# One more chunk of a feed-forward layer by seven products, on weights scaled a second time, with a new table of orders

## The chip, the cores and the metric

The kernel runs on one core of a Trainium2 chip. The metric is the device time of one execution in microseconds (us). Before the change the median of 3 runs is 268.34 us (267.95 to 268.7).

A core has engines that run side by side, each with its own list of instructions in a fixed order: TensorE (PE in the profile; its weight loads are listed apart as PEld), VectorE (DVE), ScalarE (ACT), GpSimd (POOL) and SyncE (SP), whose list here starts the DMA transfers. An engine takes the next instruction of its list only when the semaphores that this instruction names have been raised by the others. So an instruction that waits holds back everything behind it on its engine.

## The reference

Four layers work on an activation x of 2048 tokens by 512 features, in bf16: attention A, feed-forward B, then A and B again with the same weights.

```python
def _A_ref(x, wqkv, wo):                       # D = 512, 32 heads of 16
    q, k, v = ...                              # x @ wqkv, split into heads
    phi = lambda t: jnp.where(t > 0, t + 1, jnp.exp(t)) + 1e-6
    pq, pk = phi(q), phi(k)
    kv = jnp.einsum("bhsd,bhse->bhde", pk, v)
    z = jnp.einsum("bhsd->bhd", pk)
    num = jnp.einsum("bhqd,bhde->bhqe", pq, kv)
    den = jnp.einsum("bhqd,bhd->bhq", pq, z)[..., None] + 1e-6
    return ... (num / den) @ wo

def _B_ref(x, w1, w2):                         # w1 512 x 1376, w2 1376 x 512
    return jnp.maximum(x @ w1, 0) @ w2

x = x + _A_ref(_layernorm(x), wqkv, wo)        # layer 0
x = x + _B_ref(_layernorm(x), w1, w2)          # layer 1
x = x + _A_ref(_layernorm(x), wqkv, wo)        # layer 2
x = x + _B_ref(_layernorm(x), w1, w2)          # layer 3
```

The layer norm has no weights; it subtracts the mean and divides by the root of variance + 1e-5.

## The kernel before

**Tiles.** The 2048 tokens are 16 tiles of 128 (`i`), and four tiles are a chunk (`t`, 0 to 3). The 1376 hidden features are ten blocks of 128 and a rest of 96. Block `c` (0 to 4) and block `c + 5` make a block pair. PSUM, where PE writes, has eight banks of 128 x 512 f32; `alloc_bank` takes one for a piece of work. The buffer `big` is cut into units of 128 x 512 bf16: hidden features of one block and chunk, or scaled queries and their divisors in the attention layers.

**An attention layer** first takes, per chunk, keys times values (`kproj`, the features phi on ACT and DVE, then the products `g` of tokens), and at its end, called the bar here, it folds these into one matrix `Mf` per half (`GT`, `KVT`, `Mf` are the steps), computes the divisors ("dens", `ps<-big,Zc` in the profile, 32 rows), takes their reciprocal on ACT (`lnd`, `rdc`), spreads them over the rows by DMAs (`spread`, L893), multiplies the queries by them on DVE (`pqs`, L899), and multiplies by `Mf` (`fin`, `ps<-Mf,big`; the first ones are `ps<-Mf,xres`). `resid` (L748 on DVE) adds the result to x and gives the row sums; ACT squares (L754); POOL turns the sums into the layer norm's factors; DVE or ACT writes the normed tile (`norm`, L644 and L652). Then a transposing DMA started by SP (L660, `tr`) puts the chunk's rows into `Tb`, where PE reads them. The first chunk's rows are transposed by PE itself (`trp`) and copied out of PSUM by `trev`.

**A feed-forward layer** computes per chunk the hidden features (`b_h`), then sums of them (`feature_sums`, L1183 on DVE), then the output (`b_out`). The output is computed for two token tiles and two column halves together by seven products in place of eight (Strassen's idea in Winograd's form: sums of blocks are multiplied, and the seven results are added up in PSUM): class `_Pair`, with `product(k)` for k = 1 to 7, five matmuls of 256 columns each. The sums of `w2` that it needs are made once (`weight_sums`, L1152).

For the hidden features there are two forms. The plain form (`b_h_plain`) takes four matmuls of 512 columns per block, bf16. The seven-product form (`b_h_halves`) takes a block pair and the chunk's two token halves together: seven products `hp{t}_{c}_{k}` of two matmuls of 256 columns each, in f16, with sums of token blocks (`tsum`, L1031) and of weight blocks (`sw`, L1010). Product 1 goes into half a bank `Y`, product 5 into its other half; ACT copies both (`hc` into the bank `R`, `hm` into `escr`, both L1065); DVE adds the second copy to later products (half adds `ha`, L1068); a relu per block ends it (L1121 on ACT or L1122 on DVE). Which chunks take this form says `H16`: before, chunks 2 and 3 of layer 1 and all of layer 3. `H_PLAIN` gives the number of block pairs of such a chunk that stay plain.

**The weights of the f16 form.** f16 has a smaller range than bf16, so `scale_find` takes a bound of the weights and finds a power of two; `scale_weights` multiplies `w1` by it in place (`wsc0` to `wsc3`, L1003 on DVE or L1004 on ACT, each 128 x 1376) and makes the four sums `sw`. Being in place, this comes after the last plain product that reads `w1` unscaled. Residuals undo the factor.

**What sets the order.** The program adds operations one by one with what they read and write, a list of steps interleaves each layer with the next (a step names the chunk it needs and the one it provides), and `_list_schedule` then sets each engine's list before the program is built: among the next few operations of each engine it takes the one that can start first by a table of costs (`C_*`). The order in which operations are looked at is their number plus what the table `HINTS` adds for them. An operation with two forms (`add_flex`) goes to the engine that is done with it first by those costs. `OPEN_H`, `OPEN_OUT` and `ALLOC_AT` say how far one unit of seven products may start before the one ahead of it.

## Time and profile before

| what | value |
|---|---|
| median of 3 runs | 268.34 us (267.95 to 268.7) |
| the profiled execution | 267.63 us, of which 265.9 are the span |
| TensorE (PE) busy | 259.5 us, 98%, 1872 matmul records |
| VectorE (DVE) busy | 215.2 us, 81%, 555 instructions |
| ScalarE (ACT) busy | 193.7 us, 73%, 422 instructions |
| GpSimd (POOL) busy | 50.8 us, 19%, 131 instructions |
| DMA | 23.22 MB |

Rows of the profile read: line, engine, operation, out<-in by the program's names, shape, count, then busy time and the mean of one in ns, then the idle time of the engine ahead of them and what ended it. Rows of a timeline begin with the start and the duration in us of a run of like instructions. Rows of the chain begin in the same way and name the piece of work that the end of the program was followed back to. Layer 0 ends and layer 1 begins about 52.8 us into the span, layer 2 has its bar from 171 to 183 us, and layer 3 begins at about 194 us.

### The profile page before, as it was taken

To read this page: it belongs to the slowest core of one execution; us is meant where nothing else is said; L and a number is where in the kernel's file an instruction comes from. 1 tells how busy PE (TensorE), PEld (TensorE's weight loads), DVE (VectorE), ACT (ScalarE), POOL (GpSimd) and SP (SyncE) were. 2 spreads that over 40 slices of the span, in tenths; PEclk is the share of its full clock that TensorE was granted. 3 is DMA by queue.
4 is the path that set the end of the run, shared out by engine and by line. 5 is a ranking of instruction groups with operands and counts; after the bars stand their busy time and mean duration, and the time that the engine had idled before them with its cause. 6 is when DMAs were issued, how large, how long until landed. Compare 5 with 4: busy or idle time off the path is not lost.

```text
span 265.9 us, 5093 instructions
## 1 busy us (share of the span) xinstructions
PE 259.5 (98%) x1872; PEld 171.0 (64%) x1890; DVE 215.2 (81%) x555; ACT 193.7 (73%) x422; POOL 50.8 (19%) x131
## 2 busy tenths in 40 slices
...
GB/s 215 258 83 91 245 177 328 129 187 70 58 153 81 0 22 62 47 72 1 2 0 0 72 35 53 4 143 118 99 110 31 99 2 39 119 23 65 36 1 160
DMA packets 48666, 23.22 MB, mean 87 GB/s; under 512 B 38816, under 2 KB 46976, under 8 KB 48640
## 3 DMA queue, kind: packets, MB, share of 16 engines
...
q14 instruction: 11, 0.09, 0.1%
...
## 4 chain that ended last, share of the span: by engine, by line
PE 83%; DVE 6%; DMA 5%; POOL 2%; ACT 1%; issue 1%; SPq 1%; POOLq 0%; DVEq 0%
PE ps L722 83%; DMA wqkv<-in_A_wqkv_dram 4%; DVE xres L748 3%; DMA Tb<-xn 1%; DVE big L899 1%; POOL rstd L629 1%; DVE xn L644 1%; SPq L536 0%; ACT sqscr L754 0%; DVE wqkv L738 0%; DVE KVT L824 0%; POOL mean L619 0%; DVE xres L899 0%; POOL veps L627 0%; DVE big L712 0%
## 5 line engine op out<-in xcount | busy, mean ns | idle before, releaser
L1121 ACT ACTIVATE big<-ps 128x512 bf16<-128x512 f32 x62 | 35.8, 599 | 14.6 <-PE ps L722 14.1
L722 PE MATMUL ps<-Tb,w 128*128 128x256 f16 (+2 forms) x240 | 41.9, 301 | 0.0
L754 ACT ACTIVATE sqscr<-xres 128x512 bf16<-128x512 f32 x48 | 30.0, 626 | 10.7 <-DVE xres L748 10.2
L722 PE MATMUL ps<-w,big 128*128 128x256 bf16 (+5 forms) x212 | 35.8, 293 | 0.1
L722 PE MATMUL ps<-wqkv,Tb 128*128 128x512 bf16 x137 | 33.2, 379 | 1.0 <-DMA wqkv<-in_A_wqkv_dram 0.7
L704 ACT ACTIVATE big<-ps 128x512 bf16<-128x512 f32 x48 | 28.9, 606 | 5.3 <-PE ps L722 4.9
L722 PE MATMUL ps<-big,xn 128*128 128x512 bf16 (+1 forms) x155 | 30.1, 335 | 0.4 <-issue 0.2
L722 PE MATMUL ps<-xn,xin 128*128 128x256 f16 x168 | 29.9, 272 | 0.0
L722 PEld LDWEIGHTS ps<-Tb,w 128*128 128x128 f16 (+1 forms) x240 | 23.1, 98 | 9.5
L1068 DVE TENSOR_TENSOR ps<-ps,escr 128x256 f32<-128x256 f32 x56 | 23.2, 427 | 4.7 <-PE ps L722 4.6
L722 PE MATMUL ps<-Tb,wqkv 128*128 128x512 bf16 x112 | 26.9, 379 | 0.0
L706 ACT ACTIVATE escr<-ps 128x512 bf16<-128x512 f32 x44 | 26.0, 610 | 1.2 <-PE ps L722 1.2
L619 POOL TENSOR_SCALAR mean<-s 128x4 f32<-128x4 f32 (+1 forms) x13 | 4.0, 305 | 117.5 <-DVE xres L748 117.4
L722 PE MATMUL ps<-Mf,big 128*128 128x512 bf16 x108 | 24.5, 379 | 0.3
L722 PEld LDWEIGHTS ps<-wqkv,Tb 128*128 128x128 bf16 x144 | 13.8, 98 | 15.7 <-DMA wqkv<-in_A_wqkv_dram 1.2
L722 PEld LDWEIGHTS ps<-w,big 128*128 128x128 bf16 (+1 forms) x213 | 20.4, 98 | 5.0
L722 PEld LDWEIGHTS ps<-big,xn 128*128 128x128 bf16 x160 | 15.2, 98 | 12.8 <-issue 0.8
L722 PE MATMUL ps<-xin,big 128*128 128x256 bf16 x150 | 20.8, 272 | 0.0
L708 DVE TENSOR_SCALAR escr<-escr 128x512 bf16<-128x512 bf16 x52 | 14.6, 288 | 7.4 <-ACT escr L706 7.3
L715 DVE TENSOR_TENSOR big<-big,escr 128x512 bf16<-128x512 bf16 x46 | 19.0, 419 | 0.7 <-ACT big L704 0.2
L722 PEld LDWEIGHTS ps<-Mf,big 128*128 128x128 bf16 x112 | 10.7, 98 | 12.7 <-DVE big L899 0.3
L722 PEld LDWEIGHTS ps<-Tb,wqkv 128*128 128x128 bf16 x112 | 10.8, 98 | 11.4 <-DVE xres L748 0.2
(141 smaller groups left out, 494.8 us busy)
## 6 DMA issues: line engine op xcount, KB each, us to landing
...
```

The source lines that it names most:

```text
L619: g.add(POOL, lambda e: e.tensor_scalar(mean[:, sl], s1[:, sl], -INV_D, None, ALU.mult), [("s1", i) for i in tl], [("mean", i) for i in tl ...
L629: g.add(POOL, lambda e: e.tensor_tensor(rstd[:, sl], veps[:, sl], nhalf[:, 0:hi - lo], ALU.pow), [("veps", lo), ("nhalf",)], [("rstd", i) ...
L644: ts = (POOL, lambda e: e.tensor_scalar(dst, src, mean[:, i:i + 1], rstd[:, i:i + 1], ALU.add, ALU.mult), C_POOL_NORM)
L704: g.add(ACT, lambda e: e.activation(dst_ap, psv[:, b, :], ACTF.Identity, bias=1.0 + 1e-6, scale=sc), [("ps", b)] + rk, [dst_key], C_ACT_PS ...
L706: g.add(ACT, lambda e: e.activation(esc, psv[:, b, :], ACTF.Exp, scale=sc), [("ps", b)] + rk, [ekey], C_ACT_EXP + xd, name=name + "_exp")
L708: g.add(DVE, lambda e: e.tensor_scalar(esc, esc, 1.0, 1e-6, ALU.min, ALU.add), [ekey], [ekey], C_DVE_BF4X, name=name + "_em")
L715: g.add(DVE, lambda e: e.tensor_tensor(dst_ap, dst_ap, esc, ALU.max), [dst_key, ekey], [dst_key], 340.0, name=name + "_phi")
L722: last = e.matmul(o, l, r, start=st, stop=sp, skip_group_check=skip)
L748: g.add(DVE, lambda e: e.scalar_tensor_tensor(xres[:, i, :], psv[:, b, :], 0.0 if sc is None else sc, src, ALU.add if sc is None else ALU. ...
L754: g.add(ACT, lambda e: e.activation(sqscr[:, q, :], xres[:, i, :], ACTF.Square, accum_out=s2[:, i:i + 1]), [("xres", i)], [("sqscr", q), ( ...
L1068: g.add(DVE, lambda e: e.tensor_tensor(psv[:, bank, 256:512], psv[:, Y, 0:256], m5, ALU.add), [("ps", Y), ("escr", s)], [("ps", bank)], C_ ...
L1121: g.add_flex([(ACT, lambda e: e.activation(unit_ap(u), psv[:, b, :], ACTF.Relu), C_ACT_PSUM), (DVE, lambda e: e.tensor_scalar(unit_ap(u), ...
```

## The change

1. Chunk 1 of layer 1 takes the seven-product form in block pairs 0, 1 and 2; pairs 3 and 4 of it stay plain (with f16 inputs).
2. Its products need scaled weights while chunk 0 still reads the unscaled ones. A new function `scale_early` therefore writes a second, scaled copy of `w1` into units of `big` that hold nothing yet: those of chunks 2 and 3, for blocks 0 to 4 and 5 to 9, and unit 44 for the rest. It has four operations `wse` (two weight rows by five blocks of 128 each, L1049 of the new code) and one for the rest (`wser`, L1056), each for DVE or ACT. The sums `sw` are now made from this copy (L1064), ahead of chunk 0's output. The four in-place scalings `wsc` stay; all are now on DVE, where before DVE and ACT had two each.
3. The step that computes the hidden features of chunk 1 now waits in the interleaving for the last chunk of layer 0.
4. The limits `OPEN_H`, `OPEN_OUT` and `ALLOC_AT` go. Product 1 of a unit now stands behind product 5 of the unit ahead of it, in both forms, and product 5 of a hidden unit claims `R` as well.
5. `HINTS` is a wholly new table, so every engine's order changes in all layers.

In instructions: 24 matmuls of 512 columns go, 42 of 256 come. DVE gets 6 half adds, 4 token sums, 2 in-place scalings, 4 `wse` and one copy of transposed rows out of PSUM at the start, and loses 6 relus and a norm. ACT gets 6 relus, 3 `hc`, 3 `hm` and `wser`, and loses 2 in-place scalings. Lines of the code move by 12 at the front (L722 becomes L734, L748 L760) and by up to 58 further on.

The order at three places. First SP's list from the program's start, its DMA starts (`xin` is x, `wqkv` the weights; L546 is the half-matrix wq, loaded in two parts). Before:

```order
L536 DMA xin<-in_A_x_dram 128x512
L536 DMA xin<-in_A_x_dram 128x1536
L542 DMA wqkv<-in_A_wqkv_dram 128x2x512 x2
L546 DMA wqkv<-in_A_wqkv_dram 128x2x512
L536 DMA xin<-in_A_x_dram 128x1024
L536 DMA xin<-in_A_x_dram 128x2048
L536 DMA xin<-in_A_x_dram 128x1024
L536 DMA xin<-in_A_x_dram 128x2048
L546 DMA wqkv<-in_A_wqkv_dram 128x2x512
L660 DMA_TRANSPOSE Tb<-xn 128x8x128 x4
```

Now:

```order
L548 DMA xin<-in_A_x_dram 128x512
L548 DMA xin<-in_A_x_dram 128x1536
L554 DMA wqkv<-in_A_wqkv_dram 128x2x512 x2
L548 DMA xin<-in_A_x_dram 128x1024
L558 DMA wqkv<-in_A_wqkv_dram 128x2x512 x2
L548 DMA xin<-in_A_x_dram 128x1024
L548 DMA xin<-in_A_x_dram 128x2048 x2
L672 DMA_TRANSPOSE Tb<-xn 128x8x128 x4
```

The second part of wq (L546 before, L558 now) has moved from behind all loads of x to the place behind its first part, and both loads of 128x2048 stand after it.

Second, PE's list in chunk 1 of layer 1 (`w` is `w1` or `w2`, `tw` a sum of `w2`, `xin` holds sums of `w1` and `w2`, `xn` sums of features or tokens, `Tb` transposed rows). Before, from the tail of the list that overlaps the end of layer 0's output:

```order
L722 MATMUL ps<-Tb,w 128x512 x8
L722 MATMUL ps<-w,Tb 128x96 x16
L722 MATMUL ps<-Tb,w 128x512 x36
L722 MATMUL ps<-w,big 128x256 x5
L722 MATMUL ps<-tw,xn 128x256 x5
```

Now:

```order
L734 MATMUL ps<-Tb,w 128x512 x4
L734 MATMUL ps<-Tb,big 128x256 x2
L734 MATMUL ps<-Tb,big 128x512 x12
L734 MATMUL ps<-xn,xin 128x256 x2
L734 MATMUL ps<-big,Tb 128x96 x16
L734 MATMUL ps<-Tb,big 128x512 x4
L734 MATMUL ps<-Tb,big 128x256 x2
L734 MATMUL ps<-w,Tb 128x96 x16
L734 MATMUL ps<-w,big 128x256 x5
L734 MATMUL ps<-tw,xn 128x256 x5
```

The products from the second copy (`Tb,big`) and from sums (`xn,xin`) now begin among the plain blocks, and go on between the output products of chunk 0 that follow.

DVE's list ahead of that place, before (L748 residuals, L644 norms, L1122 relus, L1152 sums of `w2`, L1183 feature sums, L1031 token sums):

```order
L748 SCALAR_TENSOR_TENSOR xres,s<-ps,xin 128x512 x2
L644 TENSOR_SCALAR xn<-xres,mean,rstd 128x512 x2
L1122 TENSOR_SCALAR big<-ps 128x512 x3
L748 SCALAR_TENSOR_TENSOR xres,s<-ps,xin 128x512
L644 TENSOR_SCALAR xn<-xres,mean,rstd 128x512 x2
L1122 TENSOR_SCALAR big<-ps 128x512 x2
L1152 TENSOR_TENSOR tw<-w 128x1280
L1152 TENSOR_TENSOR xin<-w,tw 128x1280
L644 TENSOR_SCALAR xn<-xres,mean,rstd 128x512 x2
L1183 TENSOR_TENSOR xn<-big 128x1280
```

Now (L760 residual, L656 norms, L1049 the second copy, L1064 sums of it, L1040 in-place scalings, L1087 token sums):

```order
L760 SCALAR_TENSOR_TENSOR xres,s<-ps,xin 128x512
L656 TENSOR_SCALAR xn<-xres,mean,rstd 128x512 x3
L1036 TENSOR_SCALAR pw<-pw 128x1
L1035 TENSOR_SCALAR pw<-pw 128x1
L1049 TENSOR_SCALAR big<-w,pw 128x2x5x128 x2
L656 TENSOR_SCALAR xn<-xres,mean,rstd 128x512 x3
L1049 TENSOR_SCALAR big<-w,pw 128x2x5x128 x2
L1064 TENSOR_TENSOR xin<-big 128x1280
L1064 TENSOR_TENSOR xin<-xin,big 128x1280
L1040 TENSOR_SCALAR w<-w,pw 128x1376
L1087 TENSOR_TENSOR xn<-Tb 128x512
```

The relus and the feature sums that stood between the norms have made room for the second copy and its sums.

Third, PE's list at the bar of layer 2 (`big,Zc` 32 rows are the dens; `big,xn` token products; `Tb,wqkv` projections; `GT,wqkv` and `wo,KVT` the way to `Mf`). Before:

```order
L722 MATMUL ps<-ident,GT 128x1 x4
L722 MATMUL ps<-big,xn 128x512 x4
L722 MATMUL ps<-big,Zc 32x512 x12
L722 MATMUL ps<-big,xn 128x256 x8
L722 MATMUL ps<-Tb,wqkv 128x512 x4
L722 MATMUL ps<-big,xn 128x512 x4
L722 MATMUL ps<-GT,wqkv 128x128 x2
L722 MATMUL ps<-big,xn 128x256 x8
L722 MATMUL ps<-GT,wqkv 128x128 x4
L722 MATMUL ps<-Tb,wqkv 128x512 x4
L722 MATMUL ps<-GT,wqkv 128x128 x8
```

Now:

```order
L734 MATMUL ps<-ident,GT 128x1 x4
L734 MATMUL ps<-big,xn 128x256 x4
L734 MATMUL ps<-GT,wqkv 128x128 x2
L734 MATMUL ps<-big,Zc 32x512 x12
L734 MATMUL ps<-GT,wqkv 128x128 x2
L734 MATMUL ps<-big,xn 128x512 x8
L734 MATMUL ps<-GT,wqkv 128x128 x4
L734 MATMUL ps<-Tb,wqkv 128x512 x4
L734 MATMUL ps<-GT,wqkv 128x128 x6
L734 MATMUL ps<-Tb,wqkv 128x512 x4
L734 MATMUL ps<-wo,KVT 128x512 x2
```

The dens stand behind four narrow token products in place of four wide ones, and the steps towards `Mf` are spread between the token products that come after them.

The diff, cut to its core (of the table `HINTS` one line each):

```diff
-H16 = {(1, 2), (1, 3), (3, 0), (3, 1), (3, 2), (3, 3)}
+H16 = {(1, 1), (1, 2), (1, 3), (3, 0), (3, 1), (3, 2), (3, 3)}
-ALLOC_AT = 5
-OPEN_OUT = 99
-OPEN_H = 99
-H_PLAIN = {(3, 0): 2}
+H_PLAIN = {(1, 1): 2, (3, 0): 2}
-HINTS = {"0.apos": 38, "0.as_h1": -183, "0.as_h2": 580, ...
+HINTS = {"0.ainvs": 93, "0.apos": 224, "0.apows": 243, ...
...
+        def early(t):
+            return g.layer == 1 and t == 1
+
+        def w1_of(t):
+            if early(t):
+                return lambda d, c: big[:, 512 * we_unit(c) + 128 * d:512 * we_unit(c) + 128 * d + min(128, DFF - 128 * c)].bitcast(F16)
+            w = w1h if h16(t) else w1
+            return lambda d, c: w[:, d, 128 * c:min(128 * c + 128, DFF)]
+
+        def we_unit(c):
+            return 44 if c == NFC - 1 else NCH * (c % HN5) + 2 + c // HN5
+
+        def we_ap(half, d0, d1):
+            v = big[:].bitcast(F16).rearrange("p (c t d k) -> p c t d k", t=NCH, d=4, k=128)
+            return v[:, 0:HN5, 2 + half, d0:d1, :].rearrange("p c d k -> p d c k")
...
+        def scale_early():
+            for half in range(2):
+                for d in (0, 2):
+                    i_ = w1[:, d:d + 2, HD * half:HD * half + HD].rearrange("p d (c k) -> p d c k", k=128)
+                    o_ = we_ap(half, d, d + 2)
+                    g.add_flex([(DVE, lambda e, i_=i_, o_=o_: e.tensor_scalar(o_, i_, pw[:, 1:2], None, ALU.mult), C_DVE_SC),
+                                (ACT, lambda e, i_=i_, o_=o_: e.activation(o_, i_, ACTF.Copy, scale=pw[:, 1:2]), C_ACT_ABS)],
+                               [("pws",), ("w1",)], [("we", half, d)] + we_keys(half), name="wse%d%d" % (half, d))
...
-            add(1, lo[:, :, l], hi[:, :, l], ALU.add, W1S)
-            add(3, lo[:, :, f], lo[:, :, l], ALU.subtract, W1S[0:2])
...
+            add(1, ll, hl, ALU.add, [("we", 1, 0), ("we", 1, 2)] + we_keys(1))
+            add(3, lf, ll, ALU.subtract, [("we", 0, 0), ("we", 1, 0)] + we_keys(0) + we_keys(1))
...
                     op = mm_group(..., 
-                             rd + wk, [("ps", bank)], 2 * C_MM256, "hp%d_%d_%d" % (t, c, k))
-                    if k == 1 and len(h_open) >= OPEN_H:
-                        op.odeps.append(h_open[-OPEN_H])
-                    if k == 2:
-                        h_open.append(op)
+                             rd + wk, [("ps", bank)] + ([("ps", R)] if k == 5 else []), 2 * C_MM256, "hp%d_%d_%d" % (t, c, k))
+                    if k == 1:
+                        op.odeps.extend(h_open)
+                    if k == 5:
+                        h_open[:] = [op]
...
                 def h_step(t):
+                    if layer == 1 and t == 1:
+                        scale_early()
                     b_h(t, 2 if t == 0 else 1)
...
                 for t in range(NCH):
-                    steps.append((t, None, lambda t=t: h_step(t)))
+                    steps.append((NCH - 1 if layer == 1 and t == 1 else t, None, lambda t=t: h_step(t)))
                     if t >= 1:
-                        steps.append((NCH - 1 if layer == 1 and t == 1 else None, None if last_layer else t - 1, lambda t=t: o_step(t - 1)))
+                        steps.append((None, None if last_layer else t - 1, lambda t=t: o_step(t - 1)))
```

54 lines of the change are left out of this document (35 added, 19 removed), and 153 rows, old and new, of the table HINTS.

## Prediction

> **What bounds the kernel now.** I read the page first (busy time and the chain that ended last), then the windows of the feed-forward layers, then TensorE's timeline wherever the chain leaves it.
>
> ```profile
> span 265.9 us, 5093 instructions
> PE 259.5 (98%) x1872; PEld 171.0 (64%) x1890; DVE 215.2 (81%) x555; ACT 193.7 (73%) x422; POOL 50.8 (19%) x131
> PE 83%; DVE 6%; DMA 5%; POOL 2%; ACT 1%; issue 1%; SPq 1%; POOLq 0%; DVEq 0%
> ```
> ```profile
> 254.18 8.61 PE ps L722 x59
> ```
>
> TensorE (PE) is busy 98% of the span, and the chain lies on it for 83%. So time can be won in two ways only: less work for PE, or fewer of its gaps. The gaps hold little: 265.9 - 259.5 = 6.4 us, of which about 3 us lie behind the last matmul (the chain's last piece on PE, the row above, ends at 262.79). The windows, columns as in the first row, show where the two elementwise engines (DVE, ACT) are close to full beside PE.
>
> ```profile
> core 0: us, PE busy (x) PEld busy (x) DVE busy (x) ACT busy (x) POOL busy (x), PEclk, DMA share, GB/s
> 52.80:98.00 45.20, 45.14 (x314) 28.05 (x316) 42.57 (x106) 32.73 (x72) 13.84 (x32) 1.00 0.47 82
> 98.00:128.00 30.00, 29.84 (x233) 21.89 (x234) 24.77 (x64) 25.62 (x63) 6.36 (x18) 1.00 0.30 45
> 128.00:171.00 43.00, 42.79 (x277) 26.71 (x279) 31.12 (x80) 30.44 (x63) 6.57 (x18) 1.00 0.13 25
> 195.50:209.50 14.00, 13.95 (x139) 12.02 (x141) 13.73 (x34) 13.44 (x37) 3.32 (x8) 1.00 0.37 71
> ```
>
> From 52.8 to 171 PE loses almost nothing, the clock is granted in full (1.00), and DVE in the first 45.2 us has 45.20 - 42.57 = 2.6 us to spare. The last row is the stretch of layer 3 in which PE runs seven-product pairs alone: DVE has 0.27 us left of 14, and still PE is busy for 13.95.
>
> **The pairs (PE).** The price of a matmul is the distance from one row's start to the next row's, over the count; the durations overlap.
>
> ```profile
> 86.10 1.03 PE L722 MATMUL ps<-Tb,w 128*128 128x512 bf16 x4
> 86.96 0.71 PE L722 MATMUL ps<-tw,xn 128*128 128x256 bf16 x5
> ...
> 91.00 1.26 PE L722 MATMUL ps<-w,big 128*128 128x256 bf16 x10
> 92.09 0.71 PE L722 MATMUL ps<-tw,xn 128*128 128x256 bf16 x5
> ```
>
> 0.86 / 4 = 215 ns for 512 columns (216 over longer stretches), 1.09 / 10 = 109 ns for 256. Removed: 3 pairs x 2 tiles x 4 = 24 matmuls of 512 columns, 24 x 0.216 = 5.18 us. Added: 3 x 7 x 2 = 42 of 256, 42 x 0.109 = 4.58 us. Term A: -0.61 us. It holds while 256 columns cost less than 5184 / 42 = 123 ns.
>
> The Trainium skill, "TensorE: Matmul & The Clock Gate", section "Back-to-back issue gap", speaks against the change: in a stream of weight loads and matmuls it has some 131 ns for 512 columns and 81 for 128, so narrow matmuls are dear. My estimate from those two figures is 98 ns for 256 columns, and the three pairs would go from 3.14 to 4.12 us, +0.97 instead of -0.61. This trace disagrees with 131 (215 ns measured), and the measurement decides.
>
> **What the pairs cost DVE and ACT.**
>
> ```profile
> L748 DVE SCALAR_TENSOR_TENSOR xres<-ps,xin 128x512 f32<-128x512 f32 x16 | 10.4, 686 | 0.1
> L1122 DVE TENSOR_SCALAR big<-ps 128x512 bf16<-128x512 f32 x6 | 3.8, 678 | 0.0
> L1031 DVE TENSOR_TENSOR xn<-Tb 128x512 f16<-128x512 f16 x4 | 1.6, 418 | 1.7 <-DMA Tb<-xn 1.7
> L1003 DVE TENSOR_SCALAR w<-w,pw 128x1376 f16<-128x1376 bf16 x2 | 1.1, 572 | 0.0
> L1010 DVE TENSOR_TENSOR xin<-w 128x1280 f16<-128x1280 f16 x2 | 1.6, 816 | 0.0
> L1068 DVE TENSOR_TENSOR ps<-ps,escr 128x256 f32<-128x256 f32 x56 | 23.2, 427 | 4.7 <-PE ps L722 4.6
> L1065 ACT ACTIVATE ps<-ps 128x256 f32<-128x256 f32 x28 | 10.5, 384 | 1.8 <-DVE xres L748 1.2 <-DVE big L1122 0.4
> ```
>
> The column after the bar is busy us, then the mean of one in ns; a start-to-start distance on DVE is about 0.08 us less than that mean. DVE gets 6 half adds (6 x 0.34), 4 input sums (4 x 0.34), two more in-place scalings (2 x 0.49) and the four ops of the second copy; it loses 6 of its 18 relus (6 x 0.61) to ACT. No row shows the new strided, two-step copy op (2 x 640 elements). Its bounds are the scaling of 1376 elements (0.57) and the sum of 1280 (0.82); I take 0.50 of DVE's time, by the scaling, since that too reads bf16 and writes f16 with one scalar. Net: 2.0 + 1.4 + 1.0 + 2.0 - 3.7 = about +2.7 us. ACT gets 6 half copies (6 x 0.35), 6 relus (6 x 0.56), one small scaling (0.4), and loses two scalings of 1.4: about +3 us. These are off PE as long as they fit: from 52.8 to 171 DVE is free for 2.63 + 5.23 + 11.88 = 19.7 us, ACT for more.
>
> What must be there in time is the chunk's first product: the second copy and the first of its sums. On PE that is 23.4 us after the first output matmul of layer 0 (counted down the new order with the prices above). DVE's list up to there: 16 residuals x 0.61, 7 pqs x 0.335, 8 norms x 0.46, two sums of w2 (2 x 0.78), six tiny ones (6 x 0.08), four copy ops x 0.50, 19.9 us, starting about 2 us in: ready at about 22. Slack 1.4 us; each copy op would have to take 0.9 us to use it up. The remaining sums are needed at +26.2 and are done at about +23. Term E: 0 (0 to +2, the upper end being the second rival below). SP's wait on the copy does not arise: it needs no transfer. The four in-place scalings now stand behind it on DVE and are first read by chunk 2.
>
> **The start.** The new SP list issues the second half of wq two places earlier and the loads of x chunks 2 and 3 behind it.
>
> ```profile
> 6.96 5.85 DMA wqkv<-in_A_wqkv_dram
> ```
> ```profile
> 8.57 3.62 PE L722 MATMUL ps<-wqkv,Tb 128*128 128x512 bf16 x15
> 12.85 1.90 PE L722 MATMUL ps<-wqkv,Tb 128*128 128x512 bf16 x8 [0.66 <-DMA wqkv<-in_A_wqkv_dram]
> ...
> 19.34 0.60 PE L722 MATMUL ps<-big,xn 128*128 128x256 bf16 x4
> 19.78 1.03 PE L722 MATMUL ps<-wqkv,Tb 128*128 128x512 bf16 x4
> ```
>
> PE's 15 matmuls from 8.57 would be issued by 8.57 + 15 x 0.216 = 11.8, and it waits to 12.85: about 0.8 us at most above the pipeline's own distance. Issued two places up the half lands at 9 to 10 us, and this wait goes. But 19.78 stands next in line: it reads rows that come by a transposing DMA.
>
> ```profile
> 15.14 0.73 DVE L639 TENSOR_SCALAR xn<-xin,mv,rstd 128x512 bf16<-128x512 bf16 x2
> ```
> ```profile
> L660 SPq DMA_TRANSPOSE Tb<-xn x2: 1232/1284/1337, 12.9 to 15.9; - x2
> DMA to landing us min/median/max: 3.2/3.2/3.3
> ```
> ```profile
> 10.00:19.00 9.00, 8.29 (x41) 3.83 (x40) 8.71 (x30) 7.96 (x15) 2.36 (x4) 1.00 0.52 140
> ```
>
> The norms end at 15.87, the transpose is issued at 15.9 and lands at 19.2. PE used it at 19.78, so 0.6 us are free. With 0.8 us won, PE would ask at about 19.0. DVE, busy for 8.71 of 9 us there (window, columns as above), now has one copy of transposed rows out of PSUM more ahead (an estimate of 0.4 us, by the half add): the transpose lands at about 19.6. So 0.6 of the 0.8 comes back as a wait, and I take -0.1 for term B (-0.8 to +0.3). The loads of x that move back are issued two places later, which costs DVE, with its list full, nothing that I count.
>
> **The bars** (between the last key product of an attention layer and its output). Layer 0:
>
> ```profile
> 51.01 0.61 PE L722 MATMUL ps<-GT,wqkv 128*128 128x128 bf16 x8
> 51.59 0.40 PE L722 MATMUL ps<-big,Zc 128*32 128x512 bf16 x4
> 52.36 0.38 PE L722 MATMUL ps<-wo,KVT 128*128 128x512 bf16 x1 [0.38 <-DVE KVT L824]
> ```
>
> Here 0.7 us go between 51.45 and 52.36 (the rows show 8 x 0.056 and one group of 0.216 in 1.35 us), and some 0.2 at the earlier dens. The new order pulls the dens forward, but puts the first output matmul right where DVE still has an elementwise product, a cast and the first scaled query in its list, some 0.8 us late. Term C: 0.0 (-0.4 to +0.4). Layer 2:
>
> ```profile
> 179.74 0.28 PE L722 MATMUL ps<-GT,wqkv 128*128 128x128 bf16 x2
> 180.15 0.81 PE L722 MATMUL ps<-Mf,big 128*128 128x512 bf16 x3
> ...
> 194.09 1.26 PE L722 MATMUL ps<-Tb,w 128*128 128x256 f16 x10
> 195.45 0.51 PE L722 MATMUL ps<-w,Tb 128*128 128x96 f16 x8
> ```
> ```profile
> 178.70 1.42 DVE L899 TENSOR_TENSOR big<-big 128x512 bf16<-128x512 bf16 x4
> ```
> ```profile
> 192.37 3.04 DMA Tb<-xn
> ```
>
> 0.41 - 0.11 = 0.29 us are lost before 180.15, where the output waits for the scaled queries; 195.45 - 194.09 - 1.09 = 0.27 before 195.45, where the transposed rows land at 195.40; with a few tenths around the dens 0.77. The new order issues the dens, from which the scaled queries follow, some 0.7 us earlier and an output product between, and I expect 0.2 us left. Term D: -0.55 (-0.75 to +0.2).
>
> **Sum**: -0.61 - 0.1 + 0.0 - 0.55 + 0 = -1.26 us. The profiled execution took 267.63 us (span 265.9 and 1.73 around it) and stands 0.71 under the median of 268.34. So 266.4 for the like execution, 267.1 as median.
>
> **Rivals.**
> 1. *The start's gain is kept.* The transpose is issued no later than before, and PE saves the whole 0.8: -0.61 - 0.82 - 0.55 = -2.0, 266.3 us. For it: 0.6 us free at 19.78. Against: DVE's list is full from 10 to 19 us.
> 2. *Only the columns count.* The bars lose what they lose now in another place: -0.61, 267.7 us, which is within 0.3% (0.8 us), about what a measurement of this kernel can tell from no change. For it: each bar waits for chains over DVE, ACT and DMA whose length no order changes.
> 3. *DVE falls behind (slower).* From 39 to 52 us into layer 1, PE runs seven-product pairs alone: 14 half adds, each between two products on the same bank, with 0.1 to 0.3 us to spare in the new order. In the first 45 us DVE has 2.6 us free and gets 2.7 more, besides what is moved; each half add late by 0.15 us gives 14 x 0.15 - 1.26 = +0.84, 269.2 us. It decides from 0.09 us each (1.26 / 14) on. Against it: 195.5 to 209.5, where DVE is at 98% and PE loses 0.05.
> 4. *A 256-column matmul costs PE more than half of a wide one where its weight load binds.* Priced by the two mean durations below, 42 x 0.272 = 11.42 against 24 x 0.379 = 9.10, thus 5.18 x 11.42 / 9.10 = 6.51, +1.33 in place of -0.61: 269.0 us. Against it: the measured distances of 109 and 215. The rule of the skill named above would give 268.7 on the same path.
>
> ```profile
> L722 PE MATMUL ps<-wqkv,Tb 128*128 128x512 bf16 x137 | 33.2, 379 | 1.0 <-DMA wqkv<-in_A_wqkv_dram 0.7
> L722 PE MATMUL ps<-xn,xin 128*128 128x256 f16 x168 | 29.9, 272 | 0.0
> ```
>
> **How the numbers follow.** The forecast (266.6 to 267.5) 0.40, rival 1 0.12, rival 2 0.21, rival 3 0.24, rival 4 0.03. Faster: 0.40 + 0.12 = 0.52; same: 0.21 + 0.03 = 0.24; slower: 0.24. Low end: A, the start's -0.8 and both bars' lower ends, -0.61 - 0.8 - 0.4 - 0.75 = -2.56, 265.8. High end: rival 3 at 0.18 us per half add, 14 x 0.18 - 1.26 = +1.26, 269.6; beyond it half of that rival is left out.
>
> **What would show it.** Term A: 42 matmuls of 256 columns in chunk 1 of layer 1, 109 ns apart. B: no idle time on PE for wqkv near 12 us, and one before the matmuls that read chunk 1's second transpose near 19. C and D: the gaps of PE at the two bars. E: no idle PE ahead of the first product from the second copy. I am wrong if PE shows gaps released by DVE's half adds (rival 3), if the copy ops take over 0.9 us each, or if a bar grows by more than 0.4 us.

## The result and the profile after

The changed kernel takes 269.15 us (median of 22 runs, 268.4 to 271.28) where the kernel before takes 268.25 (22 runs): a ratio of 1.0036, with a 95% interval of 1.0025 to 1.0048. It is slower by about 0.9 us. The prediction was 267.1: the measured time lies inside its range of 265.8 to 269.6, but about 1.2 us of gain were forecast and a loss came.

The page of the changed kernel (profiled execution 269.28 us):

```profile
span 267.6 us, 5161 instructions
PE 261.5 (98%) x1908; PEld 172.4 (64%) x1908; DVE 220.1 (82%) x564; ACT 194.3 (73%) x434; POOL 52.8 (20%) x131
PE 79%; DVE 7%; POOL 6%; DMA 3%; ACT 2%; issue 1%; SPq 0%; POOLq 0%; DVEq 0%
```

The chain that ended last now runs over GpSimd (POOL) for 6% of the span, where it was 2%. TensorE (PE) shows more busy time although it has less to do: of before 18 matmul records are missing, of after none. So busy time does not compare the two, and I used a ledger instead: the start of a matmul on PE, less the price of all matmuls listed ahead of it. The prices are 216, 162, 109, 56 and 42 ns for 512, 384, 256, 128 and 96 columns, 220 for 96-row ones, the price of one wide matmul for four dens (they start together), and for the eight matmuls of 512 columns at the very start their own distance there, 0.43 us. What is left is the time lost up to there. The prices add up to 258.58 us before and 257.97 after, the 0.61 us of term A. The rest of the span is 261.25 us in the kernel before (265.9 less a loss of 4.65), and 260.7 in the changed one (267.6 less 6.90), as in a later run of its order (266.0 less 5.31): the form's gain arrived.

Time lost on PE, by stage (the first line is the profile of before, with its missing records allowed for; the second a later run of the same order with another list of loads, without missing records):

| kernel | to the queries of chunk 2 | bar of layer 0 | layer 1 to its first output products | to layer 2's last keys | bar of layer 2 and start of layer 3 | rest | sum |
|---|---|---|---|---|---|---|---|
| before | 2.58 | 1.09 | 0.01 | 0.10 | 0.79 | 0.08 | 4.65 |
| before, one load moved | 2.61 | 0.89 | 0.01 | 0.09 | 0.78 | 0.08 | 4.46 |
| changed | 3.00 | 1.24 | 1.42 | 0.09 | 1.08 | 0.07 | 6.90 |

The loss grew by 2.25 us and the work fell by 0.61: +1.64, against +1.7 in the spans. (This pair of profiles stands further apart than the medians, since the profile of before is a quick one, 0.6 us under its median.) The largest piece is new: 1.4 us in layer 1. PE's timeline of the changed kernel:

```profile
7.65 2.33 PE L734 MATMUL ps<-wqkv,Tb 128*128 128x512 bf16 x10 [0.88 <-DMA wqkv<-in_A_wqkv_dram]
...
52.92 1.04 PE L734 MATMUL ps<-Mf,xres 128*128 128x512 bf16 x4 [0.67 <-DVE xres L911]
...
81.66 0.39 PE L734 MATMUL ps<-Tb,big 128*128 128x256 f16 x2 [0.36 <-ACT ps L1121]
82.50 0.85 PE L734 MATMUL ps<-w,Tb 128*128 128x96 f16 x16 [0.45 <-DVE w L1040]
...
197.83 1.05 PE L734 MATMUL ps<-Tb,w 128*128 128x256 f16 x8 [0.22 <-DMA Tb<-xn]
```

The number in brackets is PE's idle time; the ledger's figure is larger, since a matmul's duration in a row is longer than its price. At 81.66 the second pair of matmuls of chunk 1 waits for ScalarE's half copy (0.53 us by the ledger), at 82.50 the rest block of chunk 2 waits for an in-place scaling on VectorE (0.62). How these come about the chain shows:

```profile
76.04 1.51 POOL rstd L641
77.55 0.07 issue
77.61 0.45 POOL nbias L645
78.06 0.02 issue
78.08 0.81 ACT xn L664
78.90 0.98 ACT big L1177 x2
79.88 0.02 issue
79.90 0.83 DVE xn L1239
80.73 0.49 DVE w L1040
81.22 0.73 DVE Tb L1239
81.95 0.50 DVE w L1040
82.45 0.05 issue
82.50 18.62 PE ps L734 x184
```

GpSimd's factors of chunk 3 release a norm (L664, tile 12) at 78.08 that stands in ScalarE's list ahead of relus; the relus release VectorE's first feature sum (L1239) at 79.90, after 1.08 us of waiting; and the last in-place scalings (L1040) stand behind the sums. In the kernel before, GpSimd's power for the same factors ran from 74.86 to 75.89:

```profile
74.53 0.25 POOL L627 TENSOR_SCALAR veps<-var 128x4 f32<-128x4 f32 x1
74.86 1.03 POOL L629 TENSOR_TENSOR rstd<-veps,nhalf 128x4 f32<-128x4 f32 x1
```

In the changed kernel it ended at 77.55. Of the 1.66 us between the two ends, about 0.6 are what PE had lost more up to there (3.00 + 1.24 less 2.58 + 1.09 in the table).

### The profile page after: what moved, and what is told of

It is laid out like the page before. It is cut to its first block, busy times and chain, and to the rows that moved or that the text cites. A ratio compares the mean times of both kernels' runs of the same rounds, so it can differ in the third digit from the quotient of the medians.

```text
span 267.6 us, 5161 instructions
## 1 busy us (share of the span) xinstructions
PE 261.5 (98%) x1908; PEld 172.4 (64%) x1908; DVE 220.1 (82%) x564; ACT 194.3 (73%) x434; POOL 52.8 (20%) x131
## 4 chain that ended last, share of the span: by engine, by line
PE 79%; DVE 7%; POOL 6%; DMA 3%; ACT 2%; issue 1%; SPq 0%; POOLq 0%; DVEq 0%
PE ps L734 79%; DVE xres L760 3%; POOL rstd L641 2%; DMA wqkv<-in_A_wqkv_dram 2%; ACT sqscr L766 1%; DMA Tb<-xn 1%; DVE big L911 1%; POOL nm L635 1%; POOL xn L656 1%; DVE xn L656 1%; POOL veps L639 1%; POOL var L637 0%; POOL nbias L645 0%; DVE xres L911 0%; DVE w L1040 0%
## 5 line engine op out<-in xcount | busy, mean ns | idle before, releaser
L1177 ACT ACTIVATE big<-ps 128x512 bf16<-128x512 f32 x68 | 38.4, 602 | 9.2 <-PE ps L734 8.8
L734 PE MATMUL ps<-w,big 128*128 128x256 bf16 (+5 forms) x213 | 37.0, 293 | 0.0
L734 PE MATMUL ps<-wqkv,Tb 128*128 128x512 bf16 x144 | 33.7, 379 | 0.9 <-DMA wqkv<-in_A_wqkv_dram 0.9
L734 PE MATMUL ps<-Tb,w 128*128 128x256 f16 (+2 forms) x200 | 33.6, 285 | 0.2 <-DMA Tb<-xn 0.2
L716 ACT ACTIVATE big<-ps 128x512 bf16<-128x512 f32 x48 | 28.9, 617 | 5.8 <-PE ps L734 5.6
L734 PE MATMUL ps<-xn,xin 128*128 128x256 f16 x186 | 32.9, 273 | 0.0
L734 PE MATMUL ps<-big,xn 128*128 128x512 bf16 (+1 forms) x160 | 31.1, 336 | 0.0
L1124 DVE TENSOR_TENSOR ps<-ps,escr 128x256 f32<-128x256 f32 x62 | 25.6, 426 | 5.8 <-PE ps L734 5.6
L734 PE MATMUL ps<-Tb,wqkv 128*128 128x512 bf16 x112 | 27.4, 379 | 0.0
L734 PE MATMUL ps<-Mf,big 128*128 128x512 bf16 x112 | 24.9, 379 | 0.0
L734 PEld LDWEIGHTS ps<-wqkv,Tb 128*128 128x128 bf16 x144 | 13.9, 98 | 16.3 <-DMA wqkv<-in_A_wqkv_dram 1.1
L734 PEld LDWEIGHTS ps<-w,big 128*128 128x128 bf16 (+1 forms) x213 | 20.3, 98 | 4.5
L734 PEld LDWEIGHTS ps<-big,xn 128*128 128x128 bf16 x160 | 15.3, 98 | 12.1 <-issue 0.4
L734 PEld LDWEIGHTS ps<-Tb,w 128*128 128x128 f16 (+1 forms) x200 | 19.1, 98 | 6.1 <-DMA Tb<-xn 0.5
L734 PE MATMUL ps<-xin,big 128*128 128x256 bf16 x150 | 21.0, 272 | 0.0
L734 PEld LDWEIGHTS ps<-xn,xin 128*128 128x128 f16 x186 | 17.4, 98 | 4.0 <-DVE ps L1124 0.3
L734 PEld LDWEIGHTS ps<-Mf,big 128*128 128x128 bf16 x112 | 10.8, 98 | 12.9 <-ACT Mf L843 0.2
```

Of the source, the lines that this page charges most:

```text
L716: g.add(ACT, lambda e: e.activation(dst_ap, psv[:, b, :], ACTF.Identity, bias=1.0 + 1e-6, scale=sc), [("ps", b)] + rk, [dst_key], C_ACT_PS ...
L734: last = e.matmul(o, l, r, start=st, stop=sp, skip_group_check=skip)
L1124: g.add(DVE, lambda e: e.tensor_tensor(psv[:, bank, 256:512], psv[:, Y, 0:256], m5, ALU.add), [("ps", Y), ("escr", s)], [("ps", bank)], C_ ...
L1177: g.add_flex([(ACT, lambda e: e.activation(unit_ap(u), psv[:, b, :], ACTF.Relu), C_ACT_PSUM), (DVE, lambda e: e.tensor_scalar(unit_ap(u), ...
```

## The experiments

In the edits, each row is an instruction as its engine's list has it; the lists were changed at the shown places alone, except where the table of orders was exchanged. Each run is compared with runs of the kernel before that were taken beside it; their medians lie between 267.76 and 268.25 us, so the ratios compare more closely than the medians do. The changed kernel's ratio is 1.0036 (1.0025 to 1.0048). The theory at first: the loss sits in a few waits that the new order makes (the places above), not in the form. The rivals: the form loads VectorE too much, and the start's loads cost nothing.

**Layer 1: scalings ahead of the sums.**

```diff
-L1040 TENSOR_SCALAR w<-w,pw 128x1376
-L1239 TENSOR_TENSOR xn<-big 128x1280
-L1040 TENSOR_SCALAR w<-w,pw 128x1376
-L1239 TENSOR_TENSOR Tb<-xn,big 128x1280
-L1040 TENSOR_SCALAR w<-w,pw 128x1376
+L1040 TENSOR_SCALAR w<-w,pw 128x1376 x3
+L1239 TENSOR_TENSOR xn<-big 128x1280
+L1239 TENSOR_TENSOR Tb<-xn,big 128x1280
```

> The changed kernel with one edit on VectorE: the last two in-place scalings (wsc2, wsc3) stand ahead of the feature sums of chunk 0 instead of among them. Theory of places (the loss sits in a few waits that the new order makes, not in the form): the 1.08 us in which VectorE waits at 78.8 for a relu takes in the two scalings, wsc3 ends at about 80 instead of 82.44, and the 0.62 us that TensorE waits for it before the rest block of chunk 2 (82.50) go; the 0.53 us before 81.66, which wait for ScalarE's copy hc1_0, stay. So about -0.5 to -0.6 us, 268.6. Rival (VectorE is overloaded by the form, so any other work is late instead): the sums come 1 us later, the wait moves to the output products or half adds, and the time stays within 0.2 us of the changed kernel's.

Measured: 268.99 us, ratio 1.0048 (1.0029 to 1.0068). The wait before the rest block went from 0.62 to none, but the first output product behind it, which needs the third feature sum, lost 0.22. Layer 1 cost 0.98 us in place of 1.42, but the time cannot be told from that of the changed kernel. The truth lay between the two guesses: one wait went, and part of it came back at the next place.

**The start's loads, put back.**

```diff
 L554 DMA wqkv<-in_A_wqkv_dram 128x2x512 x2
+L558 DMA wqkv<-in_A_wqkv_dram 128x2x512
 L548 DMA xin<-in_A_x_dram 128x1024
-L558 DMA wqkv<-in_A_wqkv_dram 128x2x512 x2
+L548 DMA xin<-in_A_x_dram 128x2048
 L548 DMA xin<-in_A_x_dram 128x1024
-L548 DMA xin<-in_A_x_dram 128x2048 x2
+L548 DMA xin<-in_A_x_dram 128x2048
+L558 DMA wqkv<-in_A_wqkv_dram 128x2x512
```

> The changed kernel with the start's list of loads in the order of the kernel before (second half of wq last). Theory: the weights wk0, issued at 2.18 us in both kernels, land at 6.6 instead of 7.6, because fewer bytes are under way beside them, and TensorE's wait of 1.05 us before its first key product goes; but the new order of TensorE wants the second half of wq at about 11.2 us and it lands at 12.8, so about 1.5 us are lost there: sum +0.3 to +0.7 us, 269.6. Rival (the landing of wk0 varies from run to run and has nothing to do with what is issued behind it): wk0 lands at 7.6 still, and the sum is +0.5 to +1.0 from the late half of wq alone, with the wait before the first key product unchanged.

Measured: 270.52 us, ratio 1.0095 (1.0081 to 1.0109), 1.4 us more than the changed kernel by the medians and 1.6 by the ratios. PE waited for the late half:

```profile
13.52 1.68 PE L734 MATMUL ps<-wqkv,Tb 128*128 128x512 bf16 x7 [2.51 <-DMA wqkv<-in_A_wqkv_dram]
```

So the new order of PE depends on the new list of loads, by more than either guess allowed. The weights wk0 landed at 5.81 us here, and the wait before the first key products was gone, as the theory had it; but the wait for the late half cost 2.68 us by the ledger where about 1.5 were expected.

**The new loads in the kernel before.** The same lists, the other way round.

```diff
-L546 DMA wqkv<-in_A_wqkv_dram 128x2x512
 L536 DMA xin<-in_A_x_dram 128x1024
-L536 DMA xin<-in_A_x_dram 128x2048
+L546 DMA wqkv<-in_A_wqkv_dram 128x2x512 x2
 L536 DMA xin<-in_A_x_dram 128x1024
-L536 DMA xin<-in_A_x_dram 128x2048
-L546 DMA wqkv<-in_A_wqkv_dram 128x2x512
+L536 DMA xin<-in_A_x_dram 128x2048 x2
```

> The kernel before, with the changed kernel's list of loads at the start and nothing else. Theory: the wait of 0.82 us for the second half of wq goes, and wk0 lands at 7.6 instead of 6.6, so that about 1 us is lost ahead of the first key product: sum 0 to +0.4 us, 268.3 to 268.7. Rival (the prediction's: the earlier half of wq costs nothing at the start): -0.5 to -0.8 us, 267.6, wk0 landing at 6.6.

Measured: 267.30 us, ratio 0.9979 (0.9967 to 0.9991). The rival held: of the 0.82 us, 0.7 came in by the medians. The weights wk0 landed at 6.73 us, 0.16 later than in the kernel before and not 1 us later. PE's timeline has no wait for weights left:

```profile
6.86 1.89 PE L722 MATMUL ps<-wqkv,Tb 128*128 128x512 bf16 x8
8.59 0.39 PE L677 MATMUL ps<-ident,xn 128*128 128x128 bf16 x4
8.81 5.34 PE L722 MATMUL ps<-wqkv,Tb 128*128 128x512 bf16 x24
13.99 3.19 PE L722 MATMUL ps<-big,xn 128*128 128x512 bf16 x16
```

**The bar of layer 0, the first query ahead of the cast.**

```diff
+L911 TENSOR_TENSOR xres<-xres,big 128x4x128 x2
+L844 CAST Mf<-ps 128x512
+L911 TENSOR_TENSOR big<-big 128x512
+L720 TENSOR_SCALAR escr<-escr 128x512
 L911 TENSOR_TENSOR xres<-xres,big 128x4x128
-L911 TENSOR_TENSOR big<-big 128x512
-L844 CAST Mf<-ps 128x512
-L720 TENSOR_SCALAR escr<-escr 128x512
-L911 TENSOR_TENSOR xres<-xres,big 128x4x128 x2
```

> The changed kernel with one edit on VectorE at the bar of layer 0: the scaled query that the first output matmul reads (pqs0_0) stands ahead of the cast of Mf, and another scaled query and an elementwise product (pqs1_0, q3_1_em) behind that cast. Theory of places: TensorE's wait of 0.83 us before the first output matmul shrinks by 0.4 to 0.5 us (the cast then ends last, at about 52.3), and 0.3 to 0.5 us arrive in the time: 268.7. Rival: what was put back (the product for chunk 3's queries, one scaled query) is late in its place, the dens of chunk 3 or the second half of an output tile wait instead, and the time stays within 0.2 us.

Measured: 269.27 us, ratio 1.0061 (1.0037 to 1.0084). The rival held. The wait before the first output matmul shrank from 0.83 to 0.57 us by the ledger, and ended with the other cast, ScalarE's; the next outputs lost 0.29 us behind the dens. The bar cost 1.12 us in place of 1.24.

```profile
52.15 1.02 PE L734 MATMUL ps<-Mf,xres 128*128 128x512 bf16 x4 [0.40 <-ACT Mf L843]
```

**Layer 1: the late norm behind the half copies (ScalarE).**

```diff
-L1177 ACTIVATE big<-ps 128x512 x3
-L664 ACTIVATE xn<-xres,nbias,rstd 128x512
-L1177 ACTIVATE big<-ps 128x512 x5
-L1121 ACTIVATE ps<-ps 128x256
-L1121 ACTIVATE escr<-ps 128x256
-L664 ACTIVATE xn<-xres,nbias,rstd 128x512
+L1177 ACTIVATE big<-ps 128x512 x8
+L1121 ACTIVATE ps<-ps 128x256
+L1121 ACTIVATE escr<-ps 128x256
+L664 ACTIVATE xn<-xres,nbias,rstd 128x512 x2
```

> The changed kernel with one instruction moved on ScalarE: the norm of tile 12 (norm12b), which waits for GpSimd's slow factors of chunk 3 until 78.08 us, stands behind the first half copies (hc1_0, hm1_0) instead of ahead of five relus and those copies. Theory (one late norm at the head of ScalarE's list is the cause of both waits in layer 1): the relus run from 76.6 on, hc1_0 is done at about 80.1, VectorE's feature sum no longer waits 1.08 us for a relu, wsc3 ends at about 81.4, and of the 0.53 + 0.62 us that TensorE waits before 81.66 and before the rest block of chunk 2, at most 0.1 are left: -0.9 to -1.1 us, 268.2. Rival (the form loads VectorE and ScalarE too much, a late norm only shows where): the waits come back at other places of the next 20 us, chunk 3's transposed rows among them, and the time stays within 0.3 us of 269.15.

Measured: median 268.58 us (12 runs), ratio 1.0036 (1.0015 to 1.0056): by the ratio it cannot be told from the changed kernel. In the trace layer 1 cost 0.67 us in place of 1.42: the wait for the half copy is gone, the one for the scaling is 0.39 by the ledger.

```profile
81.23 0.85 PE L734 MATMUL ps<-w,Tb 128*128 128x96 f16 x16 [0.23 <-DVE w L1040]
```

So, by the trace, the late norm carried half of this stage's loss, less than expected.

**Orders alone, and the form alone.** One run took chunk 1 out of the seven-product form with the new table left in, one took the old table with the new code.

```diff
-H16 = {(1, 1), (1, 2), (1, 3), (3, 0), (3, 1), (3, 2), (3, 3)}
+H16 = {(1, 2), (1, 3), (3, 0), (3, 1), (3, 2), (3, 3)}
-H_PLAIN = {(1, 1): 2, (3, 0): 2}
+H_PLAIN = {(3, 0): 2}
-            return g.layer == 1 and t == 1
+            return g.layer == 1 and t == 1 and h16(t)
```

> The changed kernel without the seven-product form in chunk 1 of layer 1 (24 wide matmuls again), with the new table of orders, the second copy of the weights (which now serves the sums alone) and the new limits left in. Theory (the form itself gains 0.61 us, the new orders lose): +0.61 us on TensorE and no wait for half copies before the rest block of chunk 2, -1.15: 268.6; the waits at the bar of layer 0 (0.8 us) as in the changed kernel, those of layer 2 in some form, since its order is worked out anew. Rival (the form is what costs): all of the loss in layer 1 goes and more, and the time falls to 268.2 or below.

```diff
-HINTS = {"0.ainvs": 93, "0.apos": 224, ...
+HINTS = {"0.apos": 38, "0.as_h1": -183, ...
```

> The changed kernel with the old table of orders: seven products in chunk 1, second copy, new limits, and the order of the kernel before where its operations are the same (the start and most of layer 0). Theory (the form gains 0.61 us where its inputs are in time): the start and the bar of layer 0 as in the kernel before, -0.61 us, and waits of 0 to 1 us in layer 1, where the new operations have no numbers in the old table: 267.4 to 268.6. Rival (the form costs by itself): TensorE waits for half adds and half copies all through chunk 1's pairs, over 1 us in sum, and the time is above 268.9.

Measured: 280.94 us (ratio 1.0485) and 296.07 us (1.1043). Neither separates form and order: between layer 1's output and the last keys of layer 2, PE lost 10.9 and 14.6 us in the two, with waits of up to 3 us at places that neither kernel has. A table of numbers fits the one list of operations that it was made for; with others, the order that comes out of it is a bad one of its own. Both times lie far from what either guess reckoned with, for that reason, and both questions had to be asked with a fixed order.

**Four moves together**: the norm behind the copies, the scalings ahead of the sums, and these two.

```diff
-L656 TENSOR_SCALAR xn<-xres,mean,rstd 128x512
-L760 SCALAR_TENSOR_TENSOR xres,s<-ps,xres 128x512
-L656 TENSOR_SCALAR xn<-xres,mean,rstd 128x512
-L760 SCALAR_TENSOR_TENSOR xres,s<-ps,xres 128x512 x5
+L656 TENSOR_SCALAR xn<-xres,mean,rstd 128x512 x2
+L760 SCALAR_TENSOR_TENSOR xres,s<-ps,xres 128x512 x6
...
+L558 DMA wqkv<-in_A_wqkv_dram 128x2x512
 L548 DMA xin<-in_A_x_dram 128x1024
-L558 DMA wqkv<-in_A_wqkv_dram 128x2x512 x2
+L558 DMA wqkv<-in_A_wqkv_dram 128x2x512
```

> The changed kernel with four edits of order together: tile 12's norm behind the half copies (ScalarE), the last two in-place scalings ahead of the feature sums (VectorE), in layer 3's approach the norm of tile 3 ahead of a residual (VectorE), and at the start the first half of wq ahead of the x rows of chunk 1 and the second half behind them (SP). Theory of places: about -1.1 us in layer 1, -0.4 at the first matmuls of layer 3 (the transposed rows land 0.6 us sooner than 197.78), -0.2 to -0.5 at the start: 267.2 to 267.6, below the kernel before by 0.6 to 1.0. Rival (waits move on as soon as one is filled): less than half of the sum arrives, 268.3 or above.

Measured: 269.29 us, ratio 1.0046 (1.0031 to 1.0061). The rival held: the waits moved on. In layer 1 the first output product now waited for the third sum; at the start of layer 3 the transposed rows came 0.87 us sooner (landing at 196.91) and the 0.40 us for them were gone, but the next matmul that needs a token sum lost 0.65:

```profile
82.78 0.72 PE L734 MATMUL ps<-w,big 128*128 128x256 bf16 x5 [0.61 <-DVE big L1239]
...
199.40 0.39 PE L734 MATMUL ps<-xn,xin 128*128 128x256 f16 x2 [0.49 <-ACT big L1177]
```

**Sums first, scalings and the rest block behind them** (with the norm behind the copies).

```diff
 L1239 TENSOR_TENSOR xn<-big 128x1280
-L1040 TENSOR_SCALAR w<-w,pw 128x1376
-L1239 TENSOR_TENSOR Tb<-xn,big 128x1280
-L1040 TENSOR_SCALAR w<-w,pw 128x1376
-L1239 TENSOR_TENSOR big<-big 128x5x256
+L1239 TENSOR_TENSOR Tb<-xn,big 128x1280
+L1239 TENSOR_TENSOR big<-big 128x5x256
+L1040 TENSOR_SCALAR w<-w,pw 128x1376 x2
...
-L734 MATMUL ps<-w,Tb 128x96 x16
-L734 MATMUL ps<-w,big 128x256 x5
-L734 MATMUL ps<-tw,xn 128x256 x5
+L734 MATMUL ps<-w,big 128x256 x5
+L734 MATMUL ps<-tw,xn 128x256 x5
+L734 MATMUL ps<-w,Tb 128x96 x16
```

> The run with tile 12's norm behind the half copies, and two edits more in layer 1: VectorE makes the first three feature sums of chunk 0 in a row and the last two in-place scalings behind them, and TensorE takes the rest block of chunk 2, which needs the scalings, behind the first two output products of chunk 0, which need the sums. Theory (in that stretch VectorE's list alone is the bound: whatever it does first, TensorE waits for the last thing it needs; only work that TensorE wants later may be put back): the third sum ends at about 81.0 and the scalings at 82.0, each where TensorE asks for it, so that of the 0.39 us left in the run before at most 0.15 are left: 268.2 to 268.4. Rival (the order of these few operations does not matter, the waits move): 268.6 as in the run before, within 0.2.

Measured: 269.43 us, ratio 1.0059 (1.0038 to 1.0080). Both guesses missed on the bad side: the first output product still waited for the sum (0.39), and with the rest block moved back, the next product found the PSUM bank that the rest block's result lies in not yet read by ScalarE (0.75).

```profile
81.11 0.72 PE L734 MATMUL ps<-w,big 128*128 128x256 bf16 x5 [0.23 <-DVE big L1239]
...
83.65 0.72 PE L734 MATMUL ps<-w,big 128*128 128x256 bf16 x5 [0.58 <-ACT hr L989]
```

**More work for VectorE ahead of the place** (with the norm behind the copies): two operations of the second copy as ten small ones each.

```diff
-L1049 TENSOR_SCALAR big<-w,pw 128x2x5x128 x2
+L1049 TENSOR_SCALAR big<-w,pw 128x128 x10
+L1049 TENSOR_SCALAR big<-w,pw 128x2x5x128
 L656 TENSOR_SCALAR xn<-xres,mean,rstd 128x512 x3
-L1049 TENSOR_SCALAR big<-w,pw 128x2x5x128 x2
+L1049 TENSOR_SCALAR big<-w,pw 128x2x5x128
+L1049 TENSOR_SCALAR big<-w,pw 128x128 x10
```

> The run with tile 12's norm behind the half copies, with more work on VectorE in front of the place: two of the four operations of the second copy are ten operations each, of one row and one block of 128, which by the start-to-start distance of small operations (0.08 to 0.12 us) make 0.8 to 1.2 us in place of 0.47, so 0.7 to 1.4 us more in sum. Theory (VectorE's list is the bound from the first residual to the third feature sum, with no slack): the third sum ends later by just that, and 0.7 to 1.2 us arrive in the time: 269.3 to 269.8. Rival (ScalarE's late norm was the whole cause, and VectorE has slack once that is away): within 0.2 us of 268.58.

Measured: 270.80 us, ratio 1.0102 (1.0081 to 1.0123). The small operations took 0.246 us each, 0.165 from start to start, so that the addition was 20 x 0.165 - 2 x 0.47 = 2.4 us and not 0.7 to 1.4. The first product of the second copy then waited:

```profile
78.34 2.98 PE L734 MATMUL ps<-Tb,big 128*128 128x256 f16 x14 [1.08 <-DVE big L1049]
```

That wait is 1.24 us by the ledger, so that 2.4 - 1.24 = 1.2 us of slack lay ahead of this product (the prediction counted 1.4). Layer 1 cost 2.55 us, 1.9 more than without the addition, and the last in-place scaling ended 1.9 us later too, counted from the same start: behind the first product there is no slack. The theory held, with more time than it had reckoned because the addition was larger.

**Less work for VectorE behind the first product.**

```diff
-L1040 TENSOR_SCALAR w<-w,pw 128x1376 x4
+L1040 TENSOR_SCALAR w<-w,pw 128x32 x4
```

> The run with tile 12's norm behind the half copies, with the four in-place scalings cut to 32 of 1376 columns each, so that most of w1 stays unscaled where chunks 2 and 3 read it: this part of the computation is left out, and VectorE has about 4 x 0.42 = 1.7 us less work at the place. Theory (VectorE's list is the bound there): the rest block of chunk 2 and the first output product find their inputs ready, the 0.39 us before them go and nothing takes their place, 268.2 (-0.3 to -0.5). Rival (waits move to a release of a PSUM bank by ScalarE, whatever VectorE does): 268.6, within 0.2.

Chunks 2 and 3 then read weights of which most are unscaled: this run leaves that part of the computation out.

Measured: 268.02 us, ratio 0.9999 (0.9986 to 1.0012), an interval that lies below the changed kernel's. Layer 1 cost 0.26 us. The theory held, against a rival that the run with the sums first had made likelier: with 1.7 us less on VectorE nothing takes the waits' place.

**The second copy cut.** Left open by then was why the norm is so late. GpSimd's small operations beside the second copy are longer than their like elsewhere. This run leaves most of the copy out, so that chunk 1's products read what lies in those units.

```diff
-L1049 TENSOR_SCALAR big<-w,pw 128x2x5x128 x2
+L1049 TENSOR_SCALAR big<-w,pw 128x2x32 x2
```

> The changed kernel with the four operations of the second copy cut to 64 of 1280 columns each, so that chunk 1's seven products and the sums read what lies in those units: this part of the computation is left out. VectorE has 4 x 0.4 = 1.6 us less work ahead of the place. Theory (the second copy on VectorE holds up GpSimd beside it, GpSimd's factors of chunk 3 then release tile 12's norm late, and that norm holds up ScalarE): GpSimd's power and sum operations next to the copy fall from 1.52 and 0.82 to about 1.03 and 0.25 us, the norm starts at about 77.0 instead of 78.08 (counted with the same start of the run), the half copy hc1_0 is in time, and both waits of TensorE in layer 1 go: -0.9 to -1.2 us against 269.15, 268.1. Rival (only VectorE's own time counts): GpSimd's operations stay as long, the wait of 0.53 for the half copy stays, only the 0.62 before the rest block of chunk 2 go: -0.4 to -0.6, 268.6.

Measured: 268.26 us, ratio 1.0017 (0.9993 to 1.0041), an interval that overlaps the changed kernel's, so the time alone does not decide. The trace does: layer 1 cost 0.33 us in place of 1.42, and both waits are gone. First GpSimd's timeline in the changed kernel, then in this run (its start lay 0.7 us earlier by the ledger):

```profile
71.25 1.52 POOL L641 TENSOR_TENSOR rstd<-veps,nhalf 128x4 f32<-128x4 f32 x1
...
75.13 0.82 POOL L639 TENSOR_SCALAR veps<-var 128x4 f32<-128x4 f32 x1
76.04 1.50 POOL L641 TENSOR_TENSOR rstd<-veps,nhalf 128x4 f32<-128x4 f32 x1
```
```profile
70.57 1.19 POOL L641 TENSOR_TENSOR rstd<-veps,nhalf 128x4 f32<-128x4 f32 x1
...
74.22 0.25 POOL L639 TENSOR_SCALAR veps<-var 128x4 f32<-128x4 f32 x1
74.55 1.44 POOL L641 TENSOR_TENSOR rstd<-veps,nhalf 128x4 f32<-128x4 f32 x1
```

The norm on ScalarE followed at 76.31 in place of 78.08, 1.1 us sooner beyond the start's difference:

```profile
76.31 0.81 ACT L664 ACTIVATE xn<-xres,nbias,rstd 128x512 f16<-128x512 f32 x1 [0.44 <-POOL nbias L645]
```

The second power kept its 1.44 us: it runs beside the two sums of weights (L1064), which stayed.

**A version faster than both: the kernel before, with the second half of wq behind the x rows of chunk 1.**

```diff
 L536 DMA xin<-in_A_x_dram 128x1024
-L536 DMA xin<-in_A_x_dram 128x2048
+L546 DMA wqkv<-in_A_wqkv_dram 128x2x512
 L536 DMA xin<-in_A_x_dram 128x1024
-L536 DMA xin<-in_A_x_dram 128x2048
-L546 DMA wqkv<-in_A_wqkv_dram 128x2x512
+L536 DMA xin<-in_A_x_dram 128x2048 x2
```

> The kernel before, with the second half of wq moved up at the start to the place behind the x rows of chunk 1 (the first half stays ahead of them), and nothing else. Theory (the wait of 0.82 us for that half goes, and neither wk0 nor the first half of wq is put back): -0.6 to -0.9 us, 267.2 on the scale where the kernel before takes 268.0, as with the changed kernel's whole list or 0.1 less. Rival (gained time comes back before the products that read the second transposed half of chunk 1, as the prediction had it): -0.1 to -0.3.

Measured: 267.23 us, ratio 0.9972 (0.9959 to 0.9985). The theory held: 0.8 us less by the medians. In its trace 0.15 us came back at 19.59, before the products that the prediction had named for it.

## Why the prediction was wrong

Of the about 2.1 us between the forecast of -1.26 and the measured +0.9, term E makes 1.4, term D 0.8 and term C 0.15 to 0.35; term B takes a part of that back. Point by point, by the ledger of the two profiles:

- **Term A (-0.61), right.** 42 x 109 ns replaced 24 x 216, and the spans less the loss differ by 0.55 us. Between 88.4 and 100.9 us, where most of chunk 1's products run, the loss by these prices grows by 0.02 us in all. By rival 4's spacing the change would have cost 1.33 us of work; nothing of that is there.
- **Term B (-0.1, -0.8 to +0.3), its working wrong.** The profile shows +0.42. The wait for the late half of wq went as foreseen, but PE lost 1.05 us before its first key products to wk0, which was issued at 2.18 us in both kernels and landed at 7.60 in place of 6.57. The row is the chain's:

```profile
2.18 5.42 DMA wqkv<-in_A_wqkv_dram
```

  That landing varies: between 5.81 and 6.57 us with the old list, between 6.13 and 7.74 with the new one. The return of the gain at the second transposed half of chunk 1, on which the prediction built, did not happen in the changed kernel. In the order of before, where the two runs with earlier loads gained 0.7 and 0.8 us by the medians and 0 and 0.15 us came back at that place, rival 1's start was nearer than the forecast. In the changed kernel's typical run the worth of the new list is an estimate from medians. The changed kernel, the run without the scalings and the run without the second copy stand +0.9, -0.05 and +0.09 us from the kernel before. Take off -0.61 for the work, the loss in layer 1 (1.42, 0.26, 0.33), +0.15 to +0.35 for the bar of layer 0 and +0.29 for the later places: a gain of 0.1 to 0.5 us is left for the start, between the forecast and rival 1.
- **Term C (0.0, -0.4 to +0.4), in its range.** The bar of layer 0 cost 1.24 us in every profile of this order but one (1.12, where its list was edited), and 1.09 and twice about 0.9 in the order of before: it grew, by 0.15 to 0.35 us.
- **Term D (-0.55), wrong.** 0.2 us were to be left at the bar of layer 2 and the start of layer 3; it was 1.08, against 0.79. Two of the three things that were to go were no waits. Of the 0.29 us ahead of 180.15, 0.22 were a missing record: the row of before has three matmuls where the list has four, and in the run of its order with one load moved, where none is missing, the ledger shows 0.08 there. And the dens cost about 0.1 us ahead of each group and 0.1 behind it in both kernels, wherever they stand. Three groups of four, which make 0.66 us by their price, in the changed kernel:

```profile
173.40 0.28 PE L734 MATMUL ps<-GT,wqkv 128*128 128x128 bf16 x2
173.60 0.83 PE L734 MATMUL ps<-big,Zc 128*32 128x512 bf16 x12
174.36 0.28 PE L734 MATMUL ps<-GT,wqkv 128*128 128x128 bf16 x2
```

  Twice 0.056 after 173.40 is 173.51, and 0.66 after 173.60 is 174.26: 0.09 and 0.10 us. What was left to win was the transposed rows' 0.27. The new order has PE ask for them 1.0 us later, counted from the dens at the end of the bar (182.18 before, 183.47 now), with four more output matmuls ahead; but the rows land 1.1 us later, at 197.78, 0.39 after PE asks:

```profile
194.75 3.04 DMA Tb<-xn
```

- **Term E (0, 0 to +2), the step that failed.** The second copy itself was priced well (0.47 us each from start to start, 0.50 taken) and was in time. What failed is the sentence that the four in-place scalings "now stand behind it on DVE and are first read by chunk 2", taken at no cost. Chunk 2's rest block reads them 0.22 us of PE's work behind chunk 1's second product of the first pair, and the feature sums that chunk 0's output needs stand in the same list. And GpSimd was not looked at: the second copy holds up its operations, which makes the factors of chunk 3 late, thus a norm on ScalarE, thus the relus and the half copies behind it. That 1.4 us lie within the term's 0 to +2 is luck: that upper end was taken from rival 3 (the text says the second), whose place was another.
- **Rival 2 (the bars lose what they lose), right about the bars.** Neither loss got smaller; both grew.
- **Rival 3 (VectorE falls behind), right in kind, wrong in place.** It laid the price on 14 half adds; those lost next to nothing, while sums, scalings and a held-up GpSimd lost 1.4 us. Its time, 269.2, was the measured one, through another sum.

None of the prediction's three signs of being wrong showed: no loss of more than 0.2 us stands beside a half add, a copy operation took 0.47 us, and no bar grew by over 0.4 us. The loss came at a place for which there was no sign.

With the second copy cut, or with the norm moved and the scalings cut, the time is about that of the kernel before (268.26 and 268.02 us), although the work is 0.6 us shorter: 0.3 us still lost in layer 1, the bars and the start of layer 3 take it back, and what the start gains with it. What makes the bars and that start longer was located, not settled: the edits tried at the bar of layer 0 and at the start of layer 3 only moved the waits, and none was tried at the bar of layer 2.
